# A chunked recurrence with soft-MoE on one core: total decay out of a longer suffix scan, softmax sums out of the activation, one step's keys at another place, masked decays on either engine

## The chip, the cores and the metric

The kernel runs on one core of a Trainium2 chip. The metric is device time in microseconds of one execution, as a median of several runs. The engines of the core have these names here: PE multiplies matrices (PEld is its weight load), DVE is the vector engine, ACT the scalar engine, POOL the general engine, and SP issues the DMAs.

## The reference

The first half is a linear recurrence over 768 positions for 4 batches and 8 heads with a head size D of 40; the second half is a soft mixture of experts on its output.

```python
def _attn_ref(r, k, v, w, a, b):
    ...
    for t in range(S):
        ...
        y[:, :, t] = np.einsum('bhd,bhde->bhe', rt, state)
        Sa = np.einsum('bhde,bhe->bhd', state, at)
        state_decay = state * wt[:, :, None, :] - np.einsum('bhd,bhe->bhde', Sa, bt)
        state = state_decay + np.einsum('bhd,bhe->bhde', vt, kt)

def _moe_ref(x, phi, w1, w2):
    logits = x @ phi
    d = np.exp(logits - logits.max(0)); d /= d.sum(0) + 1e-09
    slot_input = (d.T @ x).reshape(E, S_per_e, D)
    for e in range(E):
        slot_out[e] = np.maximum(slot_input[e] @ w1[e], 0.0) @ w2[e]
    c = np.exp(logits - logits.max(1)); c /= c.sum(1) + 1e-09
    return c @ slot_out
```

## The kernel before

The 768 positions are cut into 12 steps of 64 (`st`, C = 64). All 32 pairs of batch and head are worked on together, 3 heads of 40 channels (120 partitions) or 2 heads (80 partitions) at a time (`u` = 0, 1, 2), so that a step has 12 groups of columns.

**Preparation of a step.** `scan_s` runs products of the decays from the end of the chunk back (two scans, 128x390, into PSUM), takes from each the total decay of its six groups (`pc`, 128x6) and its reciprocal; `scan_k` scales the keys with the scan; `scan_c` runs two forward scans and scales `ah` with them, and copies them to SBUF. `bda_at` writes block-diagonal copies with ACT (`bd_mult`, three per step), `gram` multiplies keys and block-diagonal copies (PE) and masks the result (DVE), `kbtok` and `ctok_of` transpose.

**The solve.** Two steps share one triangular inverse (`solve_in`, 30 times `solve_step` with a multiplication and an addition each, `solve_out`). Each of its operations may stand on DVE or POOL.

**The chain.** `chain_v`, `chain_a`, `chain_e`, `chain_u` form the step's corrected values, `chain_s` the next state, in three parts u: four matmuls into PSUM, then a DVE multiplication with `pm`, the decays masked per head by `get_pm` (128x36), into the state ring `so_f`. Step 0's state goes to columns 1280 to 2559 of `so_f`. Each step needs the state of the step before. `y_*` forms the output of a step, `slots_*` the logits and a running softmax of two steps at a time (i = 0 to 5). `slots_b` finds the maximum and its negative `ng` and issues the Exp, `slots_c` sums the exponentials.

**The end.** `merge_m` and `merge_s` merge the running softmax of four parts, `first` multiplies with the experts' first weights, then come the second weights, the output multiplications and 16 stores.

**What sets the order.** All operations are recorded in a list, and then issued by a written table: `ORDER` gives the place of each in the program, `ENGINE` the engine of those that have two (`nc.either` is DVE or ACT, `nc.both` DVE or POOL), `BANKS` the PSUM bank of each tenant. Each engine works strictly in this order, and an operation waits for its operands. Every instruction that goes through the table is shown under one line of the source in the profile (L509), so rows are told apart by operation and shape.

The third step's keys (`kb2`) lie in the first 1536 columns of `so_f`, so 256 of them lie where part u = 0 of step 0's state is written; `loff`, which the solve of the first two steps uses, lies in `sdt`, in the tile `mem`.

## Time and profile before

| | us |
|---|---|
| runs | 368.4, 365.83, 362.71 (median 365.83) |
| profiled execution, its time | 365.54 |
| its span, first to last instruction | 363.7 |
| PE busy | 322.2 (89%) |
| DVE busy | 287.4 (79%) |
| ACT busy | 225.4 (62%) |
| POOL busy | 115.6 (32%) |
| mean granted TensorE clock | 0.961 |

The busy times are shares of the whole span; stages with different limits stand one behind the other in it, so the table alone doesn't say what bounds the time.

### The profile page before, as it was taken

Reading aid. Unit: us, or ns where it says so; the run is one execution under the profiler, and the core shown is the slowest. Engines: PE = TensorE matmul, PEld = TensorE weight load, DVE = VectorE, ACT = ScalarE, POOL = GpSimd, SP = SyncE. Lnnn points to the kernel's source line nnn. Section 1 sums busy time; section 2 is a strip of 40 time slices with the busy share of each in tenths; the row PEclk is TensorE's granted clock in tenths of the full one; section 3 lists DMA queues with packets and bytes.
Section 4 is the critical chain, followed back from the end, with each engine's and each line's share of the span. In section 5 each row is a group of like instructions: output and inputs, shape, how many; then the busy total and the mean of one; then the engine's idle time right before and its main releaser. Section 6 shows DMA issues by size and latency. Waiting matters only on the chain.

```text
span 363.7 us, 16917 instructions
## 1 busy us (share of the span) xinstructions
PE 322.2 (89%) x7425; PEld 281.5 (77%) x7425; DVE 287.4 (79%) x608; ACT 225.4 (62%) x527; POOL 115.6 (32%) x230
## 2 busy tenths in 40 slices
PE   0766867999999999999999999979979899989991
PEld 0665855899999999989889889869878788842881
DVE  5999997799998999999999998946785647564322
ACT  2699996389567597678977769851634242431341
POOL 3203403333636452543725438253240000003000
PEclk9996986899999999999999999998998999999997
DMA  7980705316166226622836636865798593897067
GB/s 245 337 248 16 241 14 159 84 51 191 35 172 205 62 77 194 196 87 77 262 104 187 195 99 203 260 205 167 187 235 230 168 295 108 268 313 250 3 192 243
DMA packets 35938, 62.42 MB, mean 172 GB/s; under 512 B 3832, under 2 KB 21368, under 8 KB 35864
## 3 DMA queue, kind: packets, MB, share of 16 engines
q1 hardware_dynamic: 35864, 61.34, 55.7%
q8 instruction: 58, 0.95, 1.1%
q14 instruction: 16, 0.13, 0.1%
HBM read 57.39 MB, written 3.93 MB: 169 GB/s over the span
## 4 chain that ended last, share of the span: by engine, by line
PE 72%; DVE 12%; issue 6%; POOL 4%; ACT 2%; DMA 1%; DVEq 0%; ACTq 0%; POOLq 0%
PE ps L509 72%; DVE wt L509 8%; POOL wt L509 4%; DVE ps L509 3%; ACT wt L509 2%; DMA wt<-in_aa_dram 1%; DVE mem L509 1%; ACT mem L509 0%; ACT old_r L509 0%; ACT mid_r L509 0%; DVE slx L509 0%; DVE old L509 0%; POOL mem L509 0%; DVE mlast L509 0%; ACT mid L509 0%
## 5 line engine op out<-in xcount | busy, mean ns | idle before, releaser
L509 PE MATMUL ps<-wt,wt 32*32 32x40 f32 (+7 forms) x2936 | 143.4, 239 | 10.5 <-issue 5.3
L509 PEld LDWEIGHTS ps<-wt,wt 32*32 32x32 f32 (+7 forms) x2936 | 131.1, 133 | 19.5 <-issue 10.2
L509 PE MATMUL ps<-wt,mem 128*64 128x40 f32 (+7 forms) x1088 | 88.0, 295 | 2.7 <-issue 2.3
L509 ACT ACTIVATE wt<-ps 32x320 f32<-32x320 f32 (+1 forms) x181 | 72.8, 402 | 19.6 <-PE ps L509 13.6
L509 PEld LDWEIGHTS ps<-wt,mem 128*32 128x32 f32 (+6 forms) x1088 | 67.3, 123 | 16.0 <-issue 9.8
L509 ACT COPY wt<-ps 32x256 f32<-32x256 f32 (+4 forms) x126 | 55.7, 458 | 18.9 <-PE ps L509 8.6
L509 POOL TENSOR_TENSOR wt<-wt 128x220 f32<-128x220 f32 (+17 forms) x107 | 49.4, 462 | 50.8 <-DVE wt L509 30.2
L509 POOL TENSOR_TENSOR wt<-wt,wt 128x108 f32<-128x108 f32 (+16 forms) x97 | 48.9, 504 | 40.2 <-DVE wt L509 31.9
L509 ACT COPY mem<-ps 128x320 f32<-128x320 f32 (+4 forms) x79 | 32.5, 430 | 46.5 <-PE ps L509 44.0
L509 PE MATMUL ps<-cs_t,wt 120*128 120x120 f32 (+4 forms) x352 | 46.7, 274 | 15.7 <-DMA cs_t<-in_consts_dram 10.0
L509 DVE TENSOR_TENSOR wt<-ps,cs_t 64x512 f32<-64x512 f32 (+1 forms) x74 | 49.3, 677 | 5.1 <-PE ps L509 4.8
L509 PEld LDWEIGHTS ps<-cs_t,wt 120*128 120x128 f32 (+4 forms) x352 | 37.5, 147 | 18.4 <-ACT wt L509 15.8
L509 PE MATMUL ps<-wt 120*64 120x192 f32 (+1 forms) x288 | 47.3, 314 | 0.0
L509 DVE TENSOR_TENSOR_SCAN ps<-wt,wt 128x390 f32<-128x390 f32 x48 | 45.5, 966 | 0.3
L509 PEld LDWEIGHTS ps<-wt 120*64 120x64 f32 (+1 forms) x288 | 36.4, 137 | 0.0
L509 DVE TENSOR_TENSOR wt<-wt,ps 128x384 f32<-128x384 f32 (+1 forms) x48 | 34.4, 740 | 0.6 <-ACT wt L509 0.5
L509 ACT ACTIVATE wt<-wt,bm_t 128x768 f32<-128x768 f32 (+1 forms) x36 | 29.1, 867 | 3.1 <-DVE wt L509 3.1
L509 DVE TENSOR_TENSOR wt<-wt,wt 128x234 f32<-128x234 f32 (+15 forms) x67 | 21.7, 324 | 5.0 <-POOL wt L509 3.6
L509 POOL TENSOR_SCALAR_AFFINE_SELECT wt<-wt 128x1024 f32<-128x1024 f32 x6 | 7.6, 1266 | 56.1 <-DVE wt L509 41.9
L509 DVE STREAM_TRANSPOSE wt<-wt 128x1024 f32<-128x1024 f32 x12 | 24.7, 2081 | 0.7 <-ACT wt L509 0.3
L509 PEld LDWEIGHTS ps<-mem,wt 32*32 32x32 f32 x1792 | 19.4, 108 | 6.3 <-ACT mem L509 3.3
L509 PE MATMUL ps<-mem,wt 32*32 32x40 f32 x1792 | 22.9, 201 | 1.4 <-ACT mem L509 0.5
(87 smaller groups left out, 323.4 us busy)
## 6 DMA issues: line engine op xcount, KB each, us to landing
wt<-in_w_dram SPq DMA_DIRECT2D x40, 256.0 KB
wt<-in_w_dram SPq DMA_DIRECT2D x32, 320.0 KB
wt<-in_kb_dram SPq DMA_DIRECT2D x24, 384.0 KB
wt<-in_ww_dram SPq DMA_DIRECT2D x12, 391.0 KB
wt<-in_aa_dram SPq DMA_DIRECT2D x24, 192.0 KB
mem<-in_vt_dram SPq DMA_DIRECT2D x12, 384.0 KB
mem<-in_rr_dram SPq DMA_DIRECT2D x12, 384.0 KB
wt<-in_vv_dram SPq DMA_DIRECT2D x12, 320.0 KB
```

The lines of the kernel that those rows point to most:

```text
L509: eng.dma_start(dst, src)
```

## The change

The code changes at four places, and the three tables are written anew.

```diff
-        one, inj = part(1, 6 * CP), part(1, NG * CP)
+        one, inj = part(1, 6 * CP + 1), part(1, NG * CP)
...
-        kb2 = gkt(so_f[:, 0:1536])
+        loff = cht(so_f[:, 0:1024])
...
+        o = taken[0]
         ppb = Ring(pht(t) for t in (part(7, 512), part(7, 512), space(512)))
         sdt = space(1280)
+        kb2 = gkt(mem[:, o:o + 1536])
...
-        loff = cht(sdt[:, 0:1024])
...
         def scan_s(st):
...
-                v = bank(f"s{st}")[:, 0:6 * CP]
-                nc.vector.tensor_tensor_scan(v[:, ::-1], w[:, 2:NG * CP + 2][:, c][:, ::-1], one[:, ::-1], 0.0, ALU.mult, ALU.add)
-                s_ps[st].append((g, gcp(v)[:, :, 0:C]))
-            for g, v in s_ps[st]:
-                nc.vector.tensor_tensor(pc[:, g], gcp(w[:, 0:NG * CP])[:, g, 1], v[:, :, 0], ALU.mult)
+                v = bank(f"s{st}")
+                x = w[:, 1 + c.start:2 + c.stop]
+                nc.vector.tensor_tensor_scan(v[:, 0:6 * CP + 1][:, ::-1], x[:, ::-1], one[:, ::-1], 0.0, ALU.mult, ALU.add)
+                s_ps[st].append((g, gcp(v[:, 1:6 * CP + 1])[:, :, 0:C]))
+                nc.either.copy(pc[:, g], gcp(v[:, 0:6 * CP])[:, :, 0])
             nc.vector.reciprocal(gcp(inj)[:, :, 0], pc)
...
         def get_pm(st):
             pm = pms.put(st)
-            nc.vector.tensor_tensor(
+            nc.both.tensor_tensor(
...
-            nc.vector.tensor_scalar(ng, mn, -1.0, None, ALU.mult)
-            nc.scalar.activation(ex, lp[:, 0:128], AF.Exp, bias=ng)
+            nc.either.copy(ng, mn, scale=-1.0)
+            ess[i] = ess_t.put(i)
+            nc.scalar.activation(ex, lp[:, 0:128], AF.Exp, bias=ng, accum_out=ess[i])
...
-            es = ess_t.put(i)
-            nc.vector.tensor_reduce(es, ex, AX.X, ALU.add)
-            ess[i] = es
```

By the new tables DVE has 590 operations where it had 608, ACT 538 where it had 526, POOL 226 as before. Of the 24 new copies of the total decay 14 stand on DVE and 10 on ACT; of the 11 `get_pm` three on DVE and eight on POOL; of the six copies of `ng` three on DVE and three on ACT. Other operations change engine as well: on DVE there are 7 copies of `scan_c` (1 before), 132 multiplications and additions of the solve (124), 9 output copies (6), 2 copies of `kbtok` (6), 5 of `chain_u` (9), 1 of `y_sd` (3).

The order of DVE around the first step's three writes of the state (the rows that write from PSUM with `mem`, 120x480 and 80x320), before and then after; `wt_70` and `wt_72` are the solve's, `ps,cs_t 64x512` is the mask of `gram`. Before:

```order
96 L509 TENSOR_TENSOR wt_74<-ps_65,cs_t 64x512
97 L509 TENSOR_TENSOR wt_73<-wt_73,ps_68 128x384
98 L509 TENSOR_TENSOR wt_70<-wt_72 128x84
99 L509 TENSOR_TENSOR wt_72<-wt_72,wt_70 128x3x28
100 L509 TENSOR_TENSOR wt_73<-wt_73,ps_67 128x384
101 L509 TENSOR_TENSOR mem<-wt_70,ps_66 128x6
102 L509 TENSOR_TENSOR wt_76<-ps_68,mem 120x480
103 L509 TENSOR_TENSOR wt_76<-ps_62,mem 80x320
104 L509 TENSOR_TENSOR wt_76<-ps_64,mem 120x480
105 L509 SCALAR_TENSOR_TENSOR ps_68<-wt_70,wt_71 128x390
```

After:

```order
90 L936 TENSOR_TENSOR mem<-ps_63,cs_t 64x512
91 L936 COPY wt_73<-ps_68 128x384
92 L936 TENSOR_TENSOR wt_74<-ps_64,cs_t 64x512
93 L936 TENSOR_TENSOR wt_73<-wt_73,ps_66 128x384
94 L936 COPY mid<-ps_63 128x320
95 L936 COPY wt_75<-ps_67 128x4x120
96 L936 TENSOR_TENSOR wt_76<-ps_63,mem 80x320
97 L936 TENSOR_TENSOR mem<-ps_62,cs_t 64x512
98 L936 COPY wt_76<-wt_72 128x16x16
99 L936 TENSOR_TENSOR wt_76<-ps_66,mem 120x480
100 L936 TENSOR_TENSOR wt_76<-ps_67,mem 120x480
```

Masks of `gram` and copies now stand ahead of and between the three writes, where the three stood one behind the other. On PE the matmuls of u = 0 and u = 2 now stand ahead of step 1's `chain_v`, behind which all three stood before.

The start of DVE's order, with the second step's scans (the last rows), before and then after. Before:

```order
15 L509 SCALAR_TENSOR_TENSOR ps_68<-wt_70,wt_71 128x390
16 L509 SCALAR_TENSOR_TENSOR ps_63<-wt_70,wt_71 128x390
17 L509 TENSOR_TENSOR mem<-wt_70,ps_68 128x6
18 L509 TENSOR_TENSOR mem<-wt_70,ps_63 128x6
19 L509 RECIPROCAL wt_71<-mem 128x12
20 L509 SCALAR_TENSOR_TENSOR ps_61<-wt_70,wt_71 128x390
```

After:

```order
16 L936 SCALAR_TENSOR_TENSOR ps_67<-wt_70,wt_71 128x391
17 L936 SCALAR_TENSOR_TENSOR ps_68<-wt_70,wt_71 128x391
18 L936 COPY mem<-ps_67 128x6
19 L936 RECIPROCAL wt_71<-mem 128x12
20 L936 SCALAR_TENSOR_TENSOR ps_62<-wt_70,wt_71 128x390
```

And ACT's order there after the change, with the other copy behind the three instructions of `bd_mult`:

```order
5 L936 ACTIVATE wt_71<-wt_74,bm_t 128x512
6 L936 ACTIVATE wt_71<-wt_74,bm_t 128x768 x2
7 L936 COPY mem<-ps_68 128x6
8 L936 COPY wt_75<-ps_66 128x4x120
```

The reciprocal on DVE reads both copies, so it now also waits for ACT's. Other things that move: the memset of `loff` in `mem` is no longer the second of POOL's large memsets, and at the end `merge_m`'s and `merge_s`' small DVE operations follow each other without others between them.

## Rows read from the trace of the kernel before

**Rows 1.** Stretches: busy us (instructions) of PE, PEld, DVE, ACT, POOL; clock; DMA share; GB/s.

```profile
0.00:62.00 62.00, 38.91 (x729) 34.54 (x729) 55.63 (x99) 47.44 (x106) 14.52 (x31) 0.89 0.57 185
62.00:101.00 39.00, 38.32 (x935) 34.43 (x935) 34.70 (x70) 24.91 (x58) 17.71 (x37) 0.95 0.31 88
101.00:229.00 128.00, 127.27 (x3099) 116.28 (x3103) 121.28 (x239) 98.77 (x230) 63.38 (x124) 1.00 0.52 152
...
235.00:320.00 85.00, 78.14 (x2039) 68.58 (x2039) 53.42 (x130) 35.28 (x87) 16.06 (x32) 0.96 0.72 209
320.00:363.70 43.70, 33.77 (x476) 22.55 (x475) 16.70 (x61) 13.27 (x33) 3.25 (x5) 0.95 0.62 197
```

**Rows 2.** Timeline of DVE around the first step's state; idle time before in brackets.

```profile
61.68 0.25 DVE L509 TENSOR_TENSOR wt<-wt 128x84 f32<-128x84 f32 x1 [1.31 <-POOL wt L509]
...
65.06 0.66 DVE L509 TENSOR_TENSOR wt<-ps,mem 120x480 f32<-120x480 f32 x1 [2.32 <-PE ps L509]
```

**Rows 3.** Timeline of PE, two of the places where it waits for "issue".

```profile
62.52 0.54 PE L509 MATMUL ps<-wt,wt 32*32 32x40 f32 x18 [1.32 <-issue]
...
245.53 0.25 PE L509 MATMUL ps<-wt,mem 128*64 128x40 f32 x2 [1.57 <-issue]
```

**Rows 4.** Waits of PE over the span: us in total, times, longest.

```profile
PE ps L509 <- issue: 8.7, 9, 1.6
```

**Rows 5.** The page's DMA queues: packets, MB, share of 16 engines.

```profile
q8 instruction: 58, 0.95, 1.1%
```

**Rows 6.** Three stretches with a low clock, columns as in Rows 1.

```profile
61.00:64.00 3.00, 1.68 (x39) 1.43 (x29) 1.03 (x4) 2.10 (x4) 1.98 (x6) 0.50 0.01 2
64.00:67.00 3.00, 3.00 (x24) 2.89 (x24) 1.15 (x2) 1.08 (x2) 0.20 (x1) 0.66 0.02 5
248.00:251.00 3.00, 3.00 (x41) 2.86 (x40) 1.21 (x4) 0.31 (x1) 0.62 (x2) 0.61 0.15 55
```

**Rows 7.** Groups of DVE's instructions by shape: count, busy us, mean ns, idle before.

```profile
L509 DVE TENSOR_TENSOR wt<-wt,ps 128x384 f32<-128x384 f32 x24 | 12.6, 544 | 0.6 <-ACT wt L509 0.5
L509 DVE COPY wt<-ps 128x480 f32<-128x480 f32 x11 | 6.7, 648 | 2.9 <-PE ps L509 2.9
...
L509 DVE TENSOR_TENSOR mem<-wt,ps 128x6 f32<-128x6 f32 x24 | 3.6, 153 | 0.1
L509 DVE TENSOR_SCALAR wt<-ps 32x320 f32<-32x320 f32 x7 | 3.4, 491 | 5.4 <-PE ps L509 4.5 <-ACT wt L509 0.9
...
L509 DVE TENSOR_TENSOR mem<-mem,bm_t 128x36 f32<-128x36 f32 x11 | 2.2, 208 | 0.0
...
L509 DVE TENSOR_TENSOR wt<-wt,wt 128x240 f32<-128x240 f32 x5 | 2.0, 402 | 0.1
...
L509 DVE TENSOR_REDUCE mem<-mem 128x1 f32<-128x128 f32 x6 | 1.6, 258 | 0.0
```

**Rows 8.** Groups of ACT's instructions by shape, columns as in Rows 7.

```profile
L509 ACT ACTIVATE wt<-ps 32x320 f32<-32x320 f32 x89 | 38.1, 428 | 12.4 <-PE ps L509 8.6 <-DVE wt L509 2.3
...
L509 ACT ACTIVATE wt<-wt,bm_t 128x768 f32<-128x768 f32 x24 | 21.7, 938 | 0.1
...
L509 ACT ACTIVATE mem<-mem 128x1 f32<-128x1 f32 x5 | 1.5, 296 | 0.0
```

**Rows 9.** Timelines of POOL and DVE at the start.

```profile
2.74 0.53 POOL L509 MEMSET mem<- 128x512 f32 x1
...
3.49 1.26 DVE L509 MEMSET wt<- 128x780 f32 x3 [3.49 <-POOL mem L509]
```

**Rows 10.** Timeline of DVE and PE in the merge at the end.

```profile
322.67 0.28 DVE L509 TENSOR_REDUCE mem<-ps 1x32 f32<-1x128 f32 x1 [0.24 <-PE ps L509]
...
323.01 0.27 DVE L509 TENSOR_REDUCE mem<-ps 128x4 f32<-128x128 f32 x1
323.21 0.20 DVE L509 TENSOR_SCALAR mem<-mem 1x128 f32<-1x128 f32 x1
...
325.04 0.64 PE L509 MATMUL ps<-cs_t,mem 128*128 128x128 f32 x4
```

## The prediction

> **What bounds the kernel now.** I read the busy time by stretch first [rows 1]. From 0 to 62 us DVE is busy 55.63 us and PE only 38.91: the preparation of the first steps and the first solve set the pace, and DVE sets theirs. From 62 to 229 us PE is the limit: 38.32 of 39 us, then 127.27 of 128. DVE is close behind there (121.28 of 128), so a wait put on DVE would soon be a wait of PE, while a relief of DVE could give no more than the 0.73 us that PE is idle in that stretch. From 235 to 320 PE is busy 78.14 of 85 with DVE at 53.42, and the end (320 to 363.7) is a chain of small operations, the experts and the stores.

> Next I looked for what PE loses while it is the limit. The timeline of DVE shows 3.6 us of idle time ahead of the first step's state, 1.31 of it for POOL and 2.32 for PE [rows 2]. PE in turn stops there for 1.32 us in the middle of step 1's `chain_v`, 64 alike matmuls, and the profile names no wait but "issue" [rows 3]. Over the span such stops are 9, 8.7 us in all [rows 4]. [...] A later stop of 1.57 us [rows 3] has a stretch at 0.61 behind it [rows 6], which costs 0.39 x 3.00 = 1.2 more: 2.7 us together.

> **The change, part by part.** *Total decay.* 24 DVE multiplications of 153 ns go [rows 7], 3.7 us; 14 copies on DVE come back at about the same (2.1), so DVE gains 1.5 us. One more column in 24 scans costs nothing that could be seen. Ten copies go to ACT. The trace shows none of 128x6 there; the bounds are DVE's 153 ns and ACT's own 128x1 instruction, 296 ns [rows 7, 8], thus 1.5 to 3.0 us on an engine with 99 of 128 us busy in the long middle. I take 2.5, off the path. What they can cost is not their length but their place, and that is the second rival. *Masked decays.* Eight of 208 ns leave DVE [rows 7], 1.7 us. POOL has 63.38 of 128 us busy [rows 1] and each result is wanted only when the state of the step before is written, so I count nothing for POOL. *Softmax sums.* Six reductions of 258 ns go [rows 7], 1.5 us, five of them where PE bounds. The accumulating Exp isn't in the trace: it costs between nothing and one more small ACT instruction, 0.3 us [rows 8], and only the last of six is on the path, so 0 to 0.3; I take 0, the Exp itself being the nearest row. `ng` gives back half a microsecond of DVE at most.

> That is 5 us less on DVE. The new table gives most of it away again: six more copies of `scan_c` on DVE (544 ns for 128x384: +3.3), eight more operations of the solve (up to 402 ns: about +2), three output copies (648 ns: +1.9, in the last stretch, where the stores hide them), against four copies each of `kbtok` (-2.6) and `chain_u` (491 ns: -2.0) and two of `y_sd` (-1.3) that go to ACT [rows 7]. DVE ends 3 to 4 us lighter, and 2 of that lie at the end or where PE alone bounds. With the 0.73 us of slack above, I count **0** for 67 to 229 us, with -0.7 and +2 (if the order is a little worse there) as ends.

> *The keys' place.* The write of u = 0 had to wait for the last reader of the third step's keys, and no longer does; nor does POOL clear `loff` in `mem` first. At the start DVE's first instruction waited 3.49 us for POOL's memset in `mem`, which takes 0.53 us and is not ahead of it any more [rows 9]. The first scan then starts some **0.5 us** earlier, and the pace of 0 to 62 is DVE's. Two loads of the third step are queued on SP behind a transfer that waits for a scan; from 0 to 62 us DMA engines are busy 0.57 of the time [rows 1], so I count nothing, and up to +1 if one comes late.

> *The first step's state.* PE now does u = 0 and u = 2 ahead of step 1's `chain_v`, and DVE has masks of `gram` and copies to do while it waits. DVE's 3.6 us of idle time can be filled, which pulls later DVE work forward. [...]

> *The end.* After the maximum is reduced at 322.67 + 0.28 = 322.95, the operation that goes on begins at 323.21, since another reduction of 0.27 stands between [rows 10]; in the new order nothing does, 0.26 less. PE has the merge's matmul ahead of four transposes that end 0.64 us after their start [rows 10], about 0.5 less, and one small Exp now stands ahead of the large one on ACT, 0.3 more [rows 8]. Sum **0.5** less, between 0 and 0.8.

> Sum, from the profiled execution: 365.54 - 0.5 - 1.5 + 0 - 0.5 = **363.0 us**. That execution lies 0.3 below the median of the runs, 365.83, and the three runs differ by 5.7, so a change of 2.5 is within what the runs differ. Two per cent of 365.83, about what a measurement of this kernel can tell from no change, are 7.3 us: faster means below 358.5, slower above 373.1.

> **The rivals.** *The stops of "issue" become fewer (faster).* They come inside rows of alike matmuls, with no operand late, and the page lists an instruction queue with 58 packets and 0.95 MB [rows 5], 16 KB each: I read the stops as the supply of PE's instructions, an estimate from these rows. Another order changes when PE runs short and what DMAs run beside. If the first place goes wholly (1.7 more than counted) and two of the later ones with their stretches (2 x 2.7), the time is 363.0 - 1.7 - 5.4 = 355.9; with one, 358.6. For it: 8.7 us is to be had there and everything is reordered. Against it: the number of instructions on PE is unchanged, and so is the number of packets.

> [...]

> *DVE waits for ACT's copies of the total decay (slower).* The reciprocal is in order on DVE; behind it stand `scan_c`'s scans and, in the middle, the solve, and everything that PE gets from them. In the second step the copy stands behind three instructions of `bd_mult`, up to 938 ns each [rows 8]. Such copies are in seven of twelve steps. With one `bd_mult` instruction ahead in each, DVE stops 7 x 0.94 = 6.6 us, and since DVE is busy 121 of 128 us there [rows 1], PE stops as long: 363.0 + 6.6 = 369.6. It decides from 2.5 us in all, 0.36 a step, at which the gains are used up (365.5); one ACT instruction of 428 ns ahead in each [rows 8] is enough for that. Over 373.1 it needs 1.45 us a step. Against it: in the middle ACT idles 29 of 128 us [rows 1], and several operations stand between a copy and the reciprocal in most of those steps.

> *The change has no effect on the end.* The work taken from DVE is replaced, the first step's stop stays with its slow stretch and the end is bound by the stores: 365.0, from the start's 0.5 alone.

> **How the numbers follow.** The forecast of 363.0, with its own range of 360 to 366, has 0.55. Fewer stops (355.9 to 358.6) have 0.20, no effect (365.0) 0.13, waits for ACT (366 to 373 and beyond) 0.12. The first rival's upper half and the runs' own scatter lie in "same": faster by over 2% 0.17, within 2% 0.78, slower by over 2% 0.05. The range is from 356.0, the far end of the first rival, to 369.5, the second with one `bd_mult` ahead.

> **What would show it.** Right: DVE's first scan near 4.3 us; less than 2 us of idle DVE between 60 and 66; PE again busy over 99% from about 66 to 229; 0.3 to 0.8 less from the last maximum to the first expert matmul; 7 to 10 stops of "issue". Wrong: waits of DVE for ACT ahead of the reciprocal of over 2.5 us in all (the second rival), under five stops (the first), or PE idle in the middle because the solve, now with eight more operations on DVE, ends late.

## The result, and the profile after

The changed kernel takes 368.26 us (median of 22 runs, 364.56 to 376.15), beside 363.31 us of the kernel before (22 runs, 358.9 to 368.4) on the same chip. The ratio is 1.0146 with a 95% interval of [1.0111, 1.0181]: slower by about 1.5%, or 5 us. Some executions of a kernel are longer than its others, mostly at a lower clock, the first profiled one of the changed kernel (376.15 us, clock 0.923) among them; medians are of all runs, ratios here and below leave those out. The forecast was 2.5 us less. The time lies inside the range that was given (356.0 to 369.5), and the change is within the 2% that had most of the chance, but its sign was wrong.

The rows of after are those of a second profiled execution of the unaltered changed kernel (the experiment `x1_after` below). It took 363.31 us (span 361.6), the low end of that kernel's runs and 2.2 us less than the profiled execution of the kernel before (365.54). So the two traces show which waits come and go, and where; the size of the loss is read from the ratios.

First the same stretches as in [rows 1], with the same columns:

```profile
0.00:62.00 62.00, 39.38 (x677) 35.22 (x678) 54.42 (x93) 44.28 (x103) 13.42 (x29) 0.84 0.53 166
62.00:101.00 39.00, 38.90 (x966) 35.45 (x966) 32.81 (x64) 28.53 (x65) 18.94 (x40) 0.95 0.37 112
101.00:229.00 128.00, 125.22 (x3096) 113.29 (x3093) 121.50 (x232) 97.06 (x233) 57.13 (x113) 1.00 0.50 152
...
235.00:320.00 85.00, 80.28 (x2162) 70.37 (x2150) 58.98 (x140) 41.50 (x106) 15.66 (x35) 1.00 0.76 229
```

The third row is the one to look at. PE bounds there in both kernels, at the full clock (1.00), and it is busy 125.22 us of 128 where it was 127.27 [rows 1]: 2.8 us of idle time on the engine that has no slack. DVE is as busy as before (121.50, before 121.28). So PE's idle time there doesn't come from more work on DVE. What PE waits for from 101 to 235 us (total, times, longest):

```profile
PE ps L936 <- DVE wt L936: 1.3, 1, 1.3
PE ps L936 <- issue: 1.2, 3, 0.7
PE ps L936 <- ACT wt L936: 0.2, 1, 0.2
```

Before, the same question gave one stop of "issue" of 0.6 us and two waits for DVE of 0.4 together. From 235 to 320 us it is the other way round: "issue" is 4.1 us there and was 6.7. Over the whole span it is now 7.8 us in 11 stops, against 8.7 in 9 [rows 4]:

```profile
PE ps L936 <- issue: 7.8, 11, 1.9
```

Two of these places, and the one that is put down to DVE, in the timeline of PE:

```profile
50.82 0.94 PE L936 MATMUL ps<-mem,wt 32*32 32x40 f32 x41 [1.90 <-issue]
...
203.55 0.30 PE L936 MATMUL ps<-cs_t,mid 128*64 128x128 f32 x1 [0.68 <-issue]
...
220.57 0.79 PE L936 MATMUL ps<-mem,wt 32*32 32x40 f32 x64
221.29 0.49 PE L936 MATMUL ps<-cs_t,wt 120*128 120x120 f32 x3
223.07 0.63 PE L936 MATMUL ps<-cs_t,wt 120*120 120x120 f32 x4 [1.28 <-DVE wt L936]
```

The stop of 1.90 us is in the start, inside step 0's `chain_v`, where the kernel before had none. The slow stretch of [rows 6] has stayed, at nearly the same clock, though PE no longer stops in it:

```profile
61.00:64.00 3.00, 3.00 (x29) 2.91 (x20) 1.04 (x4) 2.64 (x7) 2.53 (x9) 0.50 0.38 83
64.00:67.00 3.00, 3.00 (x64) 2.92 (x65) 0.94 (x3) 2.54 (x4) 2.05 (x5) 0.71 1.03 414
```

DVE at the start and around the first step's state, which answers to [rows 9] and [rows 2]:

```profile
4.52 0.71 DVE L936 MEMSET wt<- 128x780 f32 x1 [2.91 <-POOL wt L936]
5.14 0.92 DVE L936 TENSOR_TENSOR_SCAN ps<-wt,wt 128x391 f32<-128x391 f32 x1
...
63.57 0.49 DVE L936 COPY mid<-ps 128x320 f32<-128x320 f32 x1 [1.96 <-PE ps L936]
...
66.69 0.49 DVE L936 TENSOR_TENSOR wt<-ps,mem 80x320 f32<-80x320 f32 x1 [2.06 <-PE ps L936]
...
67.89 1.21 DVE L936 TENSOR_TENSOR wt<-ps,mem 120x480 f32<-120x480 f32 x2
```

At the start the wait is for POOL still (2.91 us), for another of its memsets. Around the state the copies that were to fill DVE's idle time wait for PE themselves: 1.96 + 2.06 = 4.0 us idle, where it was 3.6 [rows 2]. The third write of the state ends at 67.89 + 1.21 = 69.10.

Groups of instructions (count, busy us, mean ns, idle before) that the parts of the forecast were priced with:

```profile
L936 DVE RECIPROCAL wt<-mem 128x12 f32<-128x12 f32 x12 | 2.6, 220 | 0.3 <-ACT mem L936 0.2
L936 DVE COPY mem<-ps 128x6 f32<-128x6 f32 x14 | 2.2, 161 | 0.1
...
L936 ACT COPY mem<-ps 128x6 f32<-128x6 f32 x10 | 1.6, 167 | 0.3 <-DVE ps L936 0.3
L936 ACT ACTIVATION_READ_ACCUMULATOR mem<-ps,mem 128x1 f32 x6 | 1.2, 194 | 0.0
...
L936 POOL TENSOR_TENSOR mem<-mem,bm_t 128x36 f32<-128x36 f32 x8 | 2.2, 275 | 4.1 <-DVE ps L936 3.1 <-DVE wt L936 0.9
```

The first row is the second rival's whole effect: the reciprocals, which read the copies on ACT, wait 0.3 us in all.

### The profile page after: what moved, and what is told of

Its sections match the earlier page's. It is cut to its first block, busy times and chain, and to the rows that moved or that the text cites. A ratio compares the mean times of both kernels' runs of the same rounds, so it can differ in the third digit from the quotient of the medians.

```text
span 374.4 us, 16925 instructions
## 1 busy us (share of the span) xinstructions
PE 331.9 (89%) x7425; PEld 290.3 (78%) x7425; DVE 288.0 (77%) x590; ACT 228.3 (61%) x545; POOL 111.7 (30%) x230
## 5 line engine op out<-in xcount | busy, mean ns | idle before, releaser
L936 PE MATMUL ps<-wt,wt 32*32 32x40 f32 (+8 forms) x2912 | 139.9, 237 | 8.4 <-issue 4.9
L936 PEld LDWEIGHTS ps<-wt,wt 32*32 32x32 f32 (+8 forms) x2912 | 128.8, 132 | 15.3 <-issue 7.7
L936 PE MATMUL ps<-wt,mem 128*32 128x160 f32 (+8 forms) x1112 | 95.5, 307 | 1.6 <-issue 1.6
L936 ACT ACTIVATE wt<-ps 32x256 f32<-32x256 f32 (+1 forms) x184 | 73.8, 402 | 22.6 <-PE ps L936 19.0
L936 PEld LDWEIGHTS ps<-wt,mem 128*32 128x32 f32 (+7 forms) x1112 | 73.4, 127 | 16.7 <-issue 10.3
L936 ACT COPY wt<-ps 128x480 f32<-128x480 f32 (+4 forms) x123 | 54.7, 457 | 23.6 <-PE ps L936 15.1
L936 POOL TENSOR_TENSOR wt<-wt,wt 128x130 f32<-128x130 f32 (+15 forms) x104 | 50.8, 489 | 50.9 <-DVE wt L936 28.5
L936 ACT COPY mem<-ps 128x320 f32<-128x320 f32 (+5 forms) x91 | 35.6, 403 | 44.5 <-PE ps L936 37.0
L936 POOL TENSOR_TENSOR wt<-wt 128x168 f32<-128x168 f32 (+15 forms) x92 | 42.0, 456 | 42.3 <-DVE wt L936 18.4
L936 DVE TENSOR_TENSOR_SCAN ps<-wt,wt 128x391 f32<-128x391 f32 (+1 forms) x48 | 45.5, 972 | 1.5 <-issue 0.5
```

The lines of the kernel that those rows point to most:

```text
L936: nc.vector.memset(one, 0.0)
```

## The experiments

Ratios are to the kernel before, timed on the same chip beside it (medians 361.75, 362.32 and 362.54 us for the three groups below), with a 95% interval. Four questions stood behind them, one after the other: is it the code or the tables; is it the copies on ACT; is it the order or the choice of engines, and early or late in the program; is it the place of PE's instructions in their stream.

### Code or tables: `x1_after`, `x2_tables`, `x3_code`, `x4_pcdve`

`x1_after` is the changed kernel as it is. `x2_tables` takes back the code of the total decay, the sums, `ng` and the masked decays, and keeps the new tables and the keys' new place:

```diff
-                nc.either.copy(pc[:, g], gcp(v[:, 0:6 * CP])[:, :, 0])
+                nc.vector.tensor_tensor(pc[:, g], gcp(w[:, 0:NG * CP])[:, g, 1], v[:, :, 0], ALU.mult)
...
-            nc.scalar.activation(ex, lp[:, 0:128], AF.Exp, bias=ng, accum_out=ess[i])
+            nc.scalar.activation(ex, lp[:, 0:128], AF.Exp, bias=ng)
+            nc.vector.tensor_reduce(es, ex, AX.X, ALU.add)
```

`x3_code` is the converse: these lines the other way round in the kernel before, with its order and banks, all 24 copies on DVE and the masked decays on POOL as in the change. `x4_pcdve` is the changed kernel with its ten copies of ACT on DVE (ten digits of `ENGINE`, 1 to 0).

> The changed kernel unaltered, for a trace beside the others. Every theory expects a ratio of 1.010 to 1.018 to the kernel before. Theory A (the new order costs): PE idles some 5 us between 101 and 229 us, and DVE's waits for PE and POOL there are several times those of before. Theory B (DVE waits for ACT's copies of the total decay): waits of DVE for ACT in `mem` of 2.5 us or more.

> The changed tables and the new place of the keys, with the total decay by a DVE multiplication, the sums by a DVE reduction, the masked decays and the negatives all on DVE, as before. Theory A: 1.010 to 1.022, as slow as the change or a little slower, since DVE has 5 us more work. Theory B: 0.998 to 1.005, since no copy of the total decay is left on ACT. Theory C (the accumulating Exp costs): 1.000 to 1.010.

> The order, banks and engines of before, with the longer scan, the copies of the total decay all on DVE, the accumulated sums, and the masked decays on POOL where the change has them; the keys stay where they were. Theory A: 0.990 to 1.000, the code saves up to 5 us of DVE work and PE sets the pace. Theory B: 0.990 to 1.000 too. Theory C: 1.005 or more.

> The changed kernel with all 24 copies of the total decay on DVE, in the same order (10 were on ACT). Theory A: 1.010 to 1.020, nothing gained. Theory B: 0.998 to 1.006.

| | ratio | median us |
|---|---|---|
| x1_after | 1.0122 [1.0033, 1.0211] | 368.35 |
| x2_tables | 1.0159 [1.0076, 1.0242] | 369.01 |
| x3_code | 0.9995 [0.9948, 1.0043] | 362.12 |
| x4_pcdve | 1.0179 [1.0110, 1.0249] | 367.92 |

The code alone does nothing to the time, although it takes 2.0 us of work from DVE (285.4 us busy, before 287.4), and the tables without the code cost as much as the whole change. A part of that is `x2_tables`' own, though: it has three waits of PE for ACT and DVE in the middle (1.08, 0.77 and 0.42 us) that `x1_after` doesn't have. The second rival falls: without any copy on ACT the kernel is no faster. In `x3_code` PE is busy from 101 to 229 us as it was before:

```profile
101.00:229.00 128.00, 127.82 (x3163) 117.06 (x3167) 121.55 (x234) 100.11 (x238) 63.80 (x126) 1.00 0.51 154
```

### Order or engines, early or late: `e5_eng_before`, `e6_eng_after`, `e7_late`, `e8_early`

All four have the changed code (keys at the new place in `e5_eng_before` and `e8_early`, at the old one in the others) and mixed tables: `e5_eng_before` the changed order with before's choices of engine, `e6_eng_after` before's order with the changed choices, `e7_late` before's tables for the first 540 operations (some 105 us) and the changed ones behind, `e8_early` the changed ones for the first 534 and before's behind.

Written with a name for each table (PSUM banks of a few tenants are chosen anew where the halves meet):

```diff
-ORDER, ENGINE, BANKS = changed, changed, changed
+ORDER, ENGINE = changed, before               # e5_eng_before
+ORDER, ENGINE = before, changed               # e6_eng_after
+ORDER, ENGINE = before[:540] + changed[540:]  # e7_late
+ORDER, ENGINE = changed[:534] + before[534:]  # e8_early
```

> The changed kernel in its order and banks, but every operation that could stand on either engine before stands where it stood before (scan_c's copies mostly on ACT, eight solve operations back on POOL, and so on). Theory F (the choice of engines puts too much on DVE): 0.998 to 1.005. Theories D and E (the order itself): 1.010 to 1.020.

> The order and banks of before with the code of the change (keys at their old place) and the changed choice of engines, the ten copies of the total decay on ACT included. Theory F: 1.008 to 1.015. Theories D and E: 0.995 to 1.003.

> The order of before for the first 540 operations (up to about 105 us), then the changed order; code of the change, keys at their old place. Theory D (the changed order of the start costs): 0.996 to 1.003. Theory E (the order of the middle costs, PE waits 3 to 6 us between 101 and 235 us): 1.008 to 1.018.

> The mirror image: the changed order for the first 534 operations (up to about 105 us), then the order of before; all of the changed code. Theory D: 1.007 to 1.018, with the lag of 2.5 to 4.5 us at the third solve carried to the end. Theory E: 0.996 to 1.005.

`e5_eng_before` took 441.39 us (no ratio) and `e6_eng_after` 420.59, ratio 1.1618 [1.1553, 1.1684]. The two tables belong together: in the first, operations of POOL waited 155.1 us for DVE's values and DVE 45.3 us for POOL's, and that hides whatever either table costs by itself. The two runs tell nothing on the question. `e7_late` gave 1.0174 [1.0125, 1.0222] and `e8_early` 1.0154 [1.0099, 1.0209]: each half of the new order costs as much as the whole, so they don't add up. The second has a wait of its own at the seam, which confuses it. PE's waits from 101 to 235 us there:

```profile
PE ps L935 <- DVE mem L935: 1.8, 1, 1.8
PE ps L935 <- ACT wt L935: 0.5, 1, 0.5
```

The stops of "issue" in `e8_early` are only 4.6 us over the whole span, fewer than the 8.7 of the kernel before, so what it loses besides the seam isn't explained by them and stays open. No single place in the program was found to carry the loss. What was left to test is something that follows from the order as a whole, and the stops of "issue" were the candidate.

### The place in the stream: counting PE's instructions

The page of `x1_after` gives PE's counts and the instruction queue (packets, MB, share):

```profile
PE 321.8 (89%) x7425; PEld 282.1 (78%) x7425; DVE 287.8 (80%) x590; ACT 228.3 (63%) x545; POOL 112.0 (31%) x230
...
q8 instruction: 58, 0.95, 1.1%
```

2 x 7425 / 58 = 256 instructions of PE for a packet, or nearly 128 matmuls with their weight loads. If the packets are blocks of the stream and PE stops where one ends, its stops must lie at fixed counts of matmuls from the start, whatever these matmuls are. Windows from 0 to just ahead of a stop give the count in the first parenthesis. `x1_after`:

```profile
0.00:203.00 203.00, 179.34 (x4168) 161.85 (x4168) 183.57 (x339) 150.14 (x350) 78.70 (x163) 0.94 0.47 144
0.00:222.50 222.50, 197.57 (x4678) 178.26 (x4678) 202.61 (x373) 164.81 (x388) 88.23 (x180) 0.95 0.48 147
0.00:243.10 243.10, 217.23 (x5059) 196.45 (x5060) 221.97 (x409) 181.97 (x429) 95.11 (x195) 0.95 0.49 151
0.00:247.50 247.50, 221.13 (x5187) 199.97 (x5187) 225.26 (x420) 184.66 (x436) 96.95 (x200) 0.95 0.50 154
```

And the kernel before, two of its stops of "issue":

```profile
0.00:239.00 239.00, 213.66 (x5060) 193.25 (x5061) 220.88 (x422) 179.60 (x415) 98.14 (x197) 0.96 0.50 153
0.00:284.00 284.00, 253.91 (x6079) 228.97 (x6079) 250.51 (x499) 198.45 (x460) 112.30 (x225) 0.96 0.54 161
```

5187 - 5059 = 128, 4678 - 4168 = 510 = 4 x 127.5, and 6079 - 5187 = 892 = 7 x 127.4, across the two kernels. All counts lie within 2 of 92 + 127.4 n, two numbers fitted to them. The stop at 223.07, count 4678, which the profile puts down to DVE, is among them: it too lies at a block's end. Most blocks pass without a stop. One of 127.4 matmuls lasts 5.3 us on average from 101 to 229 (128 / 3096 x 127.4). The one ahead of the stop at 223.07 is much shorter, since 64 matmuls of 32x40 run in 0.79 us; in the window 219.30 to 221.80 of `x1_after` there are 149 in 2.5 us:

```profile
219.30:221.80 2.50, 2.49 (x149) 1.71 (x139) 2.50 (x6) 2.02 (x6) 1.27 (x3) 1.00 0.89 290
```

So the theory: PE stops where the stream's next block isn't there because the last one ran too fast, and the order of the program decides which matmuls share a block.

The traces hold the packets of the instruction queue one by one, so the stops can be set beside them. Ahead of the stop that ends at 223.07 one packet ran, from 220.5 to 221.7 us. The DMA view of `x1_after` for 219 to 221.8 us lists it:

```profile
q8 instruction: 1, 0.02, 2.6%
```

Counted from the start, packet n goes with the end at 92 + 127.4 n. In this trace, in that of the kernel before and in the four of the next section there are 51 stops of "issue" of 0.2 us or more. 48 of them lie within 3 matmuls of such an end, and at each of these PE goes on 1.1 to 1.7 us after packet n has landed; no block in the six traces begins sooner than 0.9 us after its packet. (The other three are one place, 0.58 us between 47 and 50 us, whose cause stays open.) A packet takes about 1.0 us and begins, in the median, 1.1 us after the block ahead has begun. So a short block is one way to a stop: the one ahead of 223.07 ran through in 2.41 us. The other is a packet that begins late: in `p4_before_112` a stop of 2.56 us follows a block of 4.99 us, near the mean, whose packet began only 4.7 us after the block. The 4 us that the expectations below count with are the author's estimate and no fixed limit: the block of 4.99 us had a stop behind it too.

### Moving the blocks: `p1_after_108`, `p2_before_52`, `p3_after_56`, `p4_before_112`

If that is so, small matmuls ahead of everything else must move the time of either kernel up or down without any change in the order. The kernels have a table for such fillers, `FILLS`, which was empty. An instruction of 32x32 by 32x1 shows as two matmuls in the trace.

```diff
-FILLS = {}
+FILLS = {137: (54, 4, 0)}
...
-            self.nc.tensor.matmul(bank, src, src, start=True, stop=True)
+            self.nc.tensor.matmul(bank[0:32, 0:1], src[0:32, 0:32], src[0:32, 0:1], start=True, stop=True)
...
-        nc.idle = (ex, ident, sys._getframe().f_lineno)
+        nc.idle = (one, ident, sys._getframe().f_lineno)
```

54 is for 108 matmuls ahead of the changed kernel (`p1_after_108`), 28 for 56 (`p3_after_56`), 26 for 52 ahead of the kernel before (`p2_before_52`), 56 for 112 (`p4_before_112`). 108 and 112 are 15 to 20 short of a block, 52 and 56 are a little under half of one.

> The changed kernel with 54 tiny multiplications (108 PE matmul instructions, result unused) ahead of PE's first work, where PE is idle anyway. They only shift where PE's instruction blocks of 127.4 matmuls end. Theory S (PE stops where it runs through a block in under about 4 us, before the next block of its instructions has come; the new order has such blocks at 101 to 235 us, the old one not): summing 4.0 us less each short block over the changed kernel's trace gives 10.1 us as it stands and 3.1 us with this shift, so some 7 us less: 361 us, a ratio of 0.990 to 1.002 to the kernel before, and no stop over 0.6 us between 101 and 235 us. Theory G (the order itself makes PE wait for data or DVE): 1.012 to 1.020, the stops at the same matmuls as before.

> The kernel before with 26 such multiplications (52 PE matmul instructions) ahead; order, code and data as they were. Theory S: the same sum goes from 5.0 to some 16 us, so 9 to 12 us slower, a ratio of 1.022 to 1.034, with stops between 101 and 235 us where there were next to none. Theory G: 0.997 to 1.004.

> The changed kernel with 28 such multiplications (56 PE matmul instructions) ahead. Theory S: the sum goes from 10.1 to 13.7 us, a ratio of 1.018 to 1.030 to the kernel before. Theory G: 1.012 to 1.018, as the changed kernel.

> The kernel before with 56 such multiplications (112 PE matmul instructions) ahead. Theory S: the sum goes from 5.0 to 3.6 us, a ratio of 0.993 to 1.000. Theory G: 0.998 to 1.004.

| | ratio | median us | stops of "issue", whole span (us, times) |
|---|---|---|---|
| p1_after_108 | 0.9960 [0.9916, 1.0004] | 362.61 | 6.0, 7 |
| p2_before_52 | 1.0254 [1.0193, 1.0314] | 372.33 | 14.5, 14 |
| p3_after_56 | 1.0133 [1.0085, 1.0180] | 367.57 | 8.4, 10 |
| p4_before_112 | 0.9946 [0.9906, 0.9985] | 361.50 | 6.2, 6 |

108 dummy matmuls take back the whole loss of the changed kernel, and 52 of them make the kernel before slower than the change did. Theory S has three of its four forecasts right; `p3_after_56` lies where theory G had it (1.012 to 1.018). What speaks against G are pairs that differ in the number of dummy matmuls alone and were timed beside each other: 1.0133 with 56 and 0.9960 with 108, 1.0254 with 52 and 0.9946 with 112. That some work for PE at the start helps by itself, by way of the clock, has no support either: 52 and 56 don't help, and the clock from 0 to 62 us is 0.84 in `x1_after` and in `p1_after_108`. The dummy matmuls cost nothing themselves in the changed kernel, since PE has nothing to do at the start and its first matmul begins at 8.96 in `x1_after` too; PE's timeline of `p1_after_108`:

```profile
1.39 5.91 PE L275 MATMUL ps<-wt 32*32 32x1 f32 x108 [1.39 <-DVE wt L936]
8.96 0.46 PE L936 MATMUL ps<-cs_t,wt 120*128 120x120 f32 x1 [1.66 <-ACT wt L936]
```

The middle of `p1_after_108` in the view of stretches, and the same place in PE's timeline as at 220.57 above:

```profile
101.00:229.00 128.00, 127.60 (x3124) 116.02 (x3121) 122.79 (x234) 99.28 (x237) 59.02 (x115) 1.00 0.50 154
```

```profile
219.74 0.79 PE L936 MATMUL ps<-mem,wt 32*32 32x40 f32 x64
220.46 0.91 PE L936 MATMUL ps<-cs_t,wt 120*128 120x120 f32 x7
221.20 1.05 PE L936 MATMUL ps<-wt,wt 120*128 120x192 f32 x6
```

The order is the changed one, the operands are the same, and PE is busy 127.60 us, not 125.22. After the 64 short matmuls it goes on without a pause: the "wait for DVE" of 1.28 us is gone, with nothing changed on DVE. DVE's rows show that it never was one. The multiplication that ends as those four matmuls begin in `x1_after` (222.52 + 0.54 = 223.06, first row) ends in `p1_after_108` at 221.75 + 0.54 = 222.29 (second row), when PE is past them (220.46 + 0.91 = 221.37):

```profile
222.52 0.54 DVE L936 TENSOR_TENSOR wt<-wt,ps 128x384 f32<-128x384 f32 x1
...
221.75 0.54 DVE L936 TENSOR_TENSOR wt<-wt,ps 128x384 f32<-128x384 f32 x1
```

The profiled execution of `p1_after_108` took 365.79 us, more than the median of its runs, so this trace shows that the stops of the middle are gone; the gain in time is read from the ratio.

In `p2_before_52` the middle has 120.60 us of PE instead of 127.27 [rows 1], and seven stops from 101 to 235 us where there was one:

```profile
101.00:229.00 128.00, 120.60 (x3043) 109.15 (x3037) 115.75 (x226) 91.70 (x216) 56.42 (x112) 1.00 0.48 144
```

```profile
PE ps L509 <- issue: 7.3, 7, 1.8
```

Two of them in PE's timeline, and the counts ahead of them:

```profile
108.40 0.41 PE L509 MATMUL ps<-wt,wt 96*32 96x40 f32 x21 [1.81 <-issue]
...
112.40 0.19 PE L509 MATMUL ps<-mem,wt 32*32 32x40 f32 x1 [1.27 <-issue]
```

```profile
0.00:108.20 108.20, 84.60 (x1875) 75.80 (x1876) 95.89 (x173) 74.39 (x169) 33.76 (x70) 0.92 0.47 147
0.00:112.20 112.20, 87.33 (x2003) 78.33 (x2004) 98.34 (x179) 76.92 (x175) 36.92 (x80) 0.92 0.47 147
```

1875 and 2003 are 92 + 127.4 x 14 and x 15 (1875.6 and 2003.0). With 52 matmuls put ahead, the stops stand at the same counts of the stream, which are now other matmuls of the program. `p3_after_56` was forecast too high. Its middle has 2.8 us of stops, about as much as `x1_after`'s, but at other matmuls, which is not what theory G expected: the two long ones stand at counts 2512 and 3020, the ends 19 and 23, which without the 56 are matmuls 2456 and 2964; `x1_after` stops at 4168 and 4678. `p4_before_112` beats both kernels, by 0.5% the one before; PE is busy 127.89 of the 128 us there:

```profile
101.00:229.00 128.00, 127.89 (x3138) 116.98 (x3135) 122.13 (x243) 99.99 (x234) 63.82 (x125) 1.00 0.52 155
```

## Why the prediction was wrong

**The step that failed** is the term of 0 for 67 to 229 us, with -0.7 and +2 as its ends. It weighed DVE's lighter load against the 0.73 us in which PE idled, and found nothing to win. That much holds: `x3_code`, with the lighter code alone, is at 0.9995. (In the changed kernel DVE didn't even get lighter: 287.8 us busy, before 287.4, where 3 to 4 less was forecast. By the forecast's own terms the tables gave back 1.3 of 5 us, not "most of it".) What the term left out is that a new order moves every matmul to another place in the stream, and with it the stops. PE's idle time from 101 to 235 us went from 1.0 us (0.6 + 0.4) to 2.7 in `x1_after`, an execution at the low end of its runs; `p1_after_108` has 0.2 there. By the ratios, 1.0146 and 0.9960, the shift is worth 1.9%, no less than the whole loss of 1.5%.

**The first rival had the mechanism**, the supply of PE's instructions, and had its sign wrong: it allowed for fewer stops only, and argued against itself that the number of packets is the same. Their number is the same indeed (58 in both); what changed is which matmuls stand ahead of a block's end. Over the whole span the stops of "issue" are no more in sum (7.8 and 8.7 us), so that row alone doesn't tell it: more of them now fall between 101 and 235 us (1.2 us, before 0.6), and one more there, of 1.28, goes by another name.

The stops at blocks' ends last up to 1.9 us in `x1_after`, and 52 dummy matmuls, which move them, cost 2.5% (`p2_before_52`, 1.0254).

**The first step's state**, -1.5. No run shows this term, nor the 1.7 us more that the first rival counts for the same place. The stop of 1.32 us left its place [rows 3], and one of 1.90 came at 50.82. The slow stretch stayed (0.50 and 0.71, before 0.50 and 0.66), and here PE was busy for all 3.00 us from 61 to 64 at a clock of 0.50. The third write of the state ends at 69.10, before at 67.10 + 0.66 = 67.76, as the second row below shows: 1.3 later instead of 1.5 earlier. DVE in the kernel before, its first scan and that write:

```profile
4.78 0.98 DVE L509 TENSOR_TENSOR_SCAN ps<-wt,wt 128x390 f32<-128x390 f32 x1
...
67.10 0.66 DVE L509 TENSOR_TENSOR wt<-ps,mem 120x480 f32<-120x480 f32 x1 [0.42 <-PE ps L509]
```

**The start**, -0.5. DVE still waits for POOL, only for another memset, which ends later (4.52, before 3.49 [rows 9]): the first scan starts at 5.14, where 4.3 was forecast and it was 4.78 before. That is +0.4. The step that failed here is that the memset taken out of the wait was not the last thing waited for: behind it the wait went on to the next one, up to 4.52.

**The end**, -0.5. The reduction of 1x32 is now followed by its successor after 320.91 - 320.60 = 0.31 us, before after 0.54 [rows 10]; that part, 0.23, was gained as forecast. From that reduction to the first matmul of the experts it is 325.55 - 320.60 = 4.95, before 327.39 - 322.67 = 4.72. So the gain was lost again behind it. DVE after, then PE after and PE before:

```profile
320.60 0.28 DVE L936 TENSOR_REDUCE mem<-ps 1x32 f32<-1x128 f32 x1 [0.17 <-PE ps L936]
320.91 0.22 DVE L936 TENSOR_SCALAR mem<-mem 1x128 f32<-1x128 f32 x1
```

```profile
325.55 0.64 PE L936 MATMUL ps<-wt,mem 128*32 128x512 f32 x4
```

```profile
327.39 0.64 PE L509 MATMUL ps<-wt,mem 128*32 128x512 f32 x4 [0.35 <-DVE mem L509]
```

**The signs that were named.** Of five, none was met. DVE idles 3.3 us between 60 and 66 (1.96 up to 63.57, and again from 64.63 on), where under 2 was expected. The first scan is not near 4.3 but at 5.14, PE is busy 125.22 / 128 = 97.8% and not over 99%, and the end gains nothing; there are 11 stops of "issue", where 7 to 10 were expected.

**What was right.** PE bounds the middle, and relief of DVE is worth nothing: `x3_code`, with 2.0 us less of DVE's work, is at 0.9995. The second rival was rightly held unlikely: 0.3 us of waits, where it needed 2.5. Sizes: the copy on ACT takes 167 ns (counted: 250, bounds 150 to 300), that on DVE 161 (150); the masked decay on POOL 275 ns, off the path; the accumulating Exp has a second instruction of 194 ns, within the bounds of 0 to 0.3 but not at the 0 that was taken.

**What stays open.** The traces don't add up to the loss: the middle of `x1_after` has 1.7 us more idle time than before and 2.5 more than `p1_after_108`, while the ratios say 5 and 6 to 7 us. That PE stops for its next block is read from the counts, the packets and the four shifts; no run lengthened a block without moving it, and why some packets begin late isn't known. Four shifts were tried, so the best place for either kernel isn't known; at the better of those tried the two orders are alike (0.9960 and 0.9946, with overlapping intervals).

## What to carry to other kernels

Where PE bounds and the profile shows stops of "issue", count its matmuls up to each stop: if the counts differ by multiples of one number, the time may depend on where the blocks of the stream end, and a reordering may cost or give a per cent or two by that alone, as the shifts did here (1.0133 and 0.9960, 1.0254 and 0.9946). Before a new order is judged, run it, and the old one too, with half a block and nearly a block of dummy matmuls put where PE is idle. A wait that the profile names after an engine is worth a count as well, before that engine is made faster.
